# Attention and two feed-forward networks on one core: sums of weights one step ahead, g loads into x's buffers, conversions spread

## The chip, the core and the metric

One core of a Trainium2 chip runs the whole program once. The metric is the time of one execution on the device, in microseconds (us); lower is better. The engines of the core are TensorE (PE: matrix products, its loads of weights are shown as PEld), VectorE (DVE), ScalarE (ACT), GpSimd (POOL) and SyncE (SP), which issues nearly all DMAs of this kernel. Each engine takes its instructions in the order of the program.

## What is computed

```python
def reference(q, k, v, moe_w_in, moe_w_out, moe_alpha, moe2_w_in, moe2_w_out):
    # windowed attention: 4 batches, 8 heads, 576 positions, head size 64;
    # half of the heads see 32 keys, half see 32 keys at a dilation of 4
    attn = softmax(where(mask, q @ k.T / 8, -1e9)) @ v
    x = attn as (2304 tokens, 512)
    h = x @ moe_w_in                      # 512 x 2048
    x = (max(h, 0) + alpha * min(h, 0)) @ moe_w_out    # 2048 x 512
    h = x @ moe2_w_in
    g = where(h >= 1, h, where(h <= -1, 0, (h + 1) ** 2 / 4))
    return g @ moe2_w_out
```

## The kernel before

**Numbers.** Products keep nearly float32 precision: each operand is split into a high part (fp32r, a copy on ACT) and a low part (source minus high, on DVE or POOL), and each product is three matmuls, high x low, low x high, high x high. `two` (L328) does the split. The weights arrive in another format and are converted by three DVE operations on integers (`w_make`, L307) from a staging buffer `st` filled by `w_load`.

**Tiles.** Activations lie transposed in XA (512 features, 2304 tokens). Each network goes over the tokens in tiles (L45): the first in 512, 256, 512 (the plain tiles) and 1024 tokens, the second in 1024, 1024 and 256. A tile of 1024 is a pair: its first product is done by a scheme with seven products for a 2 x 2 block (`p_h`, L544), for which sums of the quarters of w_in are needed beside the weights themselves. A pair runs eight steps; step p makes h and g for f = 2p and 2p + 1 (f is one of 16 groups of 128 hidden features): 14 groups of three matmuls, then y of the two f of the step before, 12 matmuls each. g of the first 512 tokens of the pair stays on the chip (gh, gl); that of the second 512 goes to HBM (`g_keep`, gd). After the eight steps y of the second half runs over the 16 f, with gh and gl loaded back (`g_load`) and the next tile's operands (`x_seven`) made beside it. These passages from the steps to the second half of y are called boundary 1, 2 and 3 here, after the three pairs. The last tile of 256 tokens is done like a plain one.

**What runs beside what.** The attention of batch 0 is at the start; the other 18 groups of attention run between the slots of the plain tiles (`attention_point`, STARTS, STAGES). Conversions of weights are handed out a few operations at a time (`conv`, `ops` in `slot`). w_out of the second network is converted for the f in HELD within the plain tiles and stored in HBM, and for the others in the second half of the first pair, three operations per f (L1076); a load of the next st buffer is issued when a conversion ends (`more`). Each f needs woh and wol (high and low of w_out, `wo_split`), in two buffers each.

**Sums of weights.** `w_sums` (L376) makes them on POOL: four differences of quarters (ss), then two splits, and stores the split results in HBM (kept). Those of the first network are made during plain tile 2, those of the second during the first pair's steps; for that the whole w_in is fetched again (wf). `p_weights` fetches them for the next step (`w_fetch`) and splits the weights proper (`w_split`, low part on DVE in plain tile 2, on POOL later). `p_h` calls `after(0)` behind its first product and `after(1)` at its end.

**Order.** Nothing is reordered: each engine runs what the program emits for it, in that order. Waits come from buffers: a tile with a tag waits until the earlier tile of the same tag has been read for the last time. Buffers of 0.5 MB are handed round by lists of tags (x_free, st_free, r_free), first in, first out.

Of the kernel before, what the change touches and what calls it, by code (L numbers as in the profile page):

```python
# [22 lines left out]
P = 128  # L23
# [9 lines left out]
GS = 3  # L33
# [31 lines left out]
STARTS = (1, 6, 10, 14, 18, 22, 26, 30, 36, 42, 48, 54, 60, 65, 69, 73, 77, 81)  # L65
# [5 lines left out]
HELD = [f for f in range(NF) if f < 6 or f >= NF - 2]  # L71
# [15 lines left out]
def attention_then_two_ffns(ctx: ExitStack, tc: tile.TileContext, a0, aqk, av, w1i, w1o, w2i, w2o, alpha, masks, ident, out):  # L87
# [44 lines left out]
    def a_scores(i, pool, tag, add_on_pe):  # L132
# [15 lines left out]
        s = tmp(i).tile([P, 2 * GS, KEYS], F32, tag="s", name="s")  # L148
# [37 lines left out]
    def e_exp(i):  # L186
        ps = sc_t.pop(i)
        s = tmp(i).tile([P, 2 * GS, KEYS], F32, tag="s", name="s")
# [21 lines left out]
    def a_turn(i, pool, tag):  # L210
# [4 lines left out]
        pT = tmp(i).tile([P, GS, P], F32, tag="pT", name="pT")  # L215
# [138 lines left out]

    def w_split(n, f):
        t = r_slot((n, f))
        two(t[:, 0], t[:, 1], wi[n[0], f], nc.vector if n == PLAIN[2] or (n == PAIRS[0] and f < 2) else nc.gpsimd)
# [11 lines left out]

# [6 lines left out]
    def w_sums(ph, p):  # L376

        on = nc.gpsimd
        t, own = [], {}

        def fetch():
            own["tag"] = x_free.pop(0)
            own["w"] = pools[own["tag"]].tile([P, 2, DM], F32, tag=own["tag"], name="wf")
            nc.sync.dma_start(own["w"], whole[ph, 0, p])

        def quarter(i):
            w = (halves[p] if ph == 0 else own["w"])[:, i // 2]
            return w[:, (i % 2) * HW:(i % 2 + 1) * HW]

        def s12():  # L390
            t.append(ss_p.tile([P, 4, HW], F32, tag="ss", name="ss"))
            on.tensor_tensor(t[0][:, 0], quarter(3), quarter(2), ALU.add)
            on.tensor_tensor(t[0][:, 1], t[0][:, 0], quarter(0), ALU.subtract)

        def s34():
            on.tensor_tensor(t[0][:, 2], quarter(0), quarter(3), ALU.subtract)
            on.tensor_tensor(t[0][:, 3], quarter(1), t[0][:, 1], ALU.subtract)

        def keep(j):
            src = t[0][:, 2 * j - 2:2 * j].rearrange("p a b -> p (a b)")  # L400
            tag = x_free.pop(0)
            r = pools[tag].tile([P, 2, DM], F32R, tag=tag, name="wr")
            two(r[:, 0], r[:, 1], src, on)

            def store():
                kept[ph, p, j] = kept_p.tile([P, 2, DM], F32, tag=f"k{ph}_{p}_{j}", name="kept")
                nc.sync.dma_start(kept[ph, p, j], r.bitcast(F32))
                x_free.append(tag)

            later.append(store)  # L410

        def over():
            x_free.append(own["tag"])

        def save():
            d = kept_p.tile([P, 2, DM], F32, tag=f"fi_{p}", name="whole")
            nc.sync.dma_start(d, halves[p])
            whole[0, 0, p] = d

        if ph == 0:  # L420
            return [(s12, s34, save), (lambda: keep(1), lambda: keep(2), lambda: x_free.append(f"i{p}"))]
        return [(fetch,), (s12, s34, over), (lambda: keep(1), lambda: keep(2))]

    def w_fetch(key, n, p, j):
        t = r_slot(key)
        nc.sync.dma_start(t.bitcast(F32), kept[n[0], p, j])
        return t

    def p_weights(n, p, i):

        w_split(n, 2 * p + i)
        wt[n, p, 1 + i] = w_fetch((n, p, 1 + i), n, p, 1 + i)
# [70 lines left out]

    def wo_split(key, f):
# [39 lines left out]
    def p_h(q, p, after):  # L544
# [4 lines left out]
        r = [wt.pop(k) for k in ((n, 2 * p), (n, p, 1), (n, p, 2), (n, 2 * p + 1))]  # L549
# [59 lines left out]
        top(1, 1)  # L609
        product(d, 3, 0, 6, False)  # L610
# [8 lines left out]
        low(1, 1)  # L619
        top(0, 1)  # L620
        low(1, 0)
        low(0, 1)
        for k in ((n, 2 * p), (n, p, 1), (n, p, 2), (n, 2 * p + 1)):
            r_done(k)
        if p == NF // 2 - 1:
            x_free.extend(x_tags.pop(n))
        after(1)
# [7 lines left out]
    def g_load(n, f):  # L635
        hi = g_p.tile([P, TW], F32R, tag="gh", name="gh", bufs=4)
        lo = g_p.tile([P, TW], F32R, tag="gl", name="gl", bufs=4)
# [31 lines left out]
    def f_y(key, f):  # L669
# [13 lines left out]
        for c in range(NC):  # L683
# [4 lines left out]
            nc.tensor.matmul(o, wh[:, cs], gl[:, :w], start=False, stop=(f == NF - 1))  # L688
        if f == NF - 1:
# [18 lines left out]
    with tc.manual_schedule(), ExitStack() as late:  # L708
# [3 lines left out]
        e_in = [sp.tile([P, QK + GS * 4 * DS], F32, name=f"e_in{i}") for i in range(NGB)]  # L712

# [128 lines left out]
        def attention_point():  # L842
            nonlocal point, nxt
            for i in list(at):
                k = point - at[i]
                stages = STAGES[2 if 2 * NF <= at[i] < 4 * NF else i > NGB]
# [36 lines left out]
        sums = [w_sums(0, p) for p in range(NF // 2)]  # L883
        pend_2 = [(1, f, 0) for f in range(NF)] + [(1, f, 1) for f in HELD]
        after_n = dict(zip(order, order[1:] + [None]))

        def slot(n, f, k):
# [14 lines left out]
            if n in PLAIN[:2] and f == NF - 1:  # L902
                for c in range(NC):
                    x_split(nn, c)
            if k in (0, 1):
# [3 lines left out]
            elif n != LAST:  # L909
                ops = 3  # L910
# [12 lines left out]
            if n == PLAIN[2]:  # L923
                for x in sums[f // 2][f % 2]:
                    x()
                    if f < NF - 1:
                        flush()
# [6 lines left out]
            if n == PLAIN[2]:  # L934
                if f == NF // 2:
                    turn = iter(range(1 << 30))
                    x_work.extend(x_seven(nn, lambda: ps_a.tile([P, TW], F32, tag="w" if nxt < NG or at else "wa"[next(turn) % 2], name="room")))
                if f >= NF // 2:
                    more_x((2 if f < READY - 1 else 0) if f < READY else 5 if f < NF - 1 else len(x_work))
                if f == NF - 4:  # L940
                    w_base(0, 0)
                if f == NF - 3:
                    p_weights(nn, 0, 0)
                if f == NF - 1:
                    p_weights(nn, 0, 1)
                    w_base(0, 1)
                    flush()
# [12 lines left out]
        for n in PLAIN:  # L960
            for f in range(NF):
# [4 lines left out]
                if n == PLAIN[0] and f == NF - 1:  # L966
                    st_free.append(x_free.pop())
                    more()
                if n == PLAIN[1] and f == NF - 4:
                    spare += [0, 0]  # L970
                if n == PLAIN[2] and f == READY - 1:
                    assert nxt == NG and not at
                    x_free.extend(pools_q)
                if n == PLAIN[2] and f == NF // 2 - 1:
                    assert not pend_w and not todo and not cv, (pend_w, todo)
                    x_free.extend(st_free)
                    st_free.clear()

        second = [w_sums(1, p) for p in range(NF // 2)]

        def step(q, p):
            n = PAIRS[q]
            split_pending()

            def after(i):
                if p + 1 < NF // 2:
                    p_weights(n, p + 1, i)
                if i and p + 2 < NF // 2:
# [185 lines left out]
```

## Times and profile before

| | us |
|---|---|
| median of 3 runs | 914.38 |
| the 3 runs | 910.52, 914.38, 914.49 |
| profiled execution | 910.34 |
| its span | 908.5 |

| engine | busy us | share of the span |
|---|---|---|
| PE | 846.0 | 93% |
| PEld | 693.6 | 76% |
| DVE | 564.2 | 62% |
| POOL | 467.3 | 51% |
| ACT | 435.6 | 48% |

The span is what the profile covers, from the first instruction to the last. The mean granted clock of PE over it is 0.981 of full speed. Plain tile 1 runs from about 146 to 207 us of the span, plain tile 2 to about 318, the first pair's steps to 442, boundary 1 and the second half of y to 505; the second pair's boundary is at 625, the third's at 800.

### The profile page before, as it was taken

What the parts mean: (1) busy time and instruction counts of PE and PEld (TensorE: products, weight loads), DVE (VectorE), ACT (ScalarE), POOL (GpSimd) and SP (SyncE); (2) the same over time, 40 slices, a digit from 0 to 9 for tenths busy, and PEclk for the clock granted to TensorE, in tenths of its full rate; (3) what the DMA queues carried; (4) which work ended last, traced back from release to release, by engine and by line L of the source; (5) the groups of instructions that cost most, each with busy time, mean ns of one, the idle gap of its engine ahead of it and who ended that gap; (6) DMA issues with size and microseconds to landing.
All of it is one profiled execution on the core that took longest, in us unless ns stands there. A gap on an engine that the chain in (4) does not pass through costs nothing.

```text
span 908.5 us, 14621 instructions
## 1 busy us (share of the span) xinstructions
PE 846.0 (93%) x5328; PEld 693.6 (76%) x5330; DVE 564.2 (62%) x931; ACT 435.6 (48%) x809; POOL 467.3 (51%) x397
## 2 busy tenths in 40 slices
PE   6889998997999989999778999997999999969998
PEld 3667777886677868888566888886778888858898
DVE  4788886897776776565427777776317767630143
ACT  3545444554555564645424445453334545433365
POOL 3455554663657747676747233332473242327576
PEclk9999999999999999999979999999899999999999
DMA  7877736895773566775589654533674644256430
GB/s 283 251 228 227 216 104 216 253 273 149 254 246 147 183 250 248 269 299 219 188 298 318 252 186 170 184 127 106 223 255 146 226 172 175 94 191 238 161 106 24
DMA packets 73031, 185.23 MB, mean 204 GB/s; under 512 B 7552, under 2 KB 15360, under 8 KB 72960
## 3 DMA queue, kind: packets, MB, share of 16 engines
q1 hardware_dynamic: 72672, 184.14, 58.8%
q8 instruction: 42, 0.69, 0.3%
q14 instruction: 29, 0.24, 0.1%
q10 hardware_dynamic: 288, 0.16, 0.1%
HBM read 127.13 MB, written 57.15 MB: 203 GB/s over the span
## 4 chain that ended last, share of the span: by engine, by line
PE 65%; issue 9%; DVE 9%; POOL 7%; ACT 5%; DMA 4%; SPq 0%; ACTq 0%; POOLq 0%; DVEq 0%
PE y L686 11%; PE y L688 10%; PE y L687 10%; PE h_ps L559 6%; PE h_ps L561 6%; PE h_ps L560 6%; PE h_ps L529 4%; PE h_ps L531 4%; PE h_ps L530 4%; POOL wol L330 3%; POOL wr L330 2%; PE o_ps L225 2%; ACT wr L329 2%; DMA gh<-gd 1%; PE s_ps L147 1%
## 5 line engine op out<-in xcount | busy, mean ns | idle before, releaser
L330 POOL TENSOR_TENSOR wol<-wo,woh 128x512 fp32r<-128x512 f32 x159 | 205.9, 1303 | 145.3 <-ACT woh L329 144.6
L686 PE MATMUL y<-gh,wol 128*128 128x512 f32 (+1 forms) x636 | 242.8, 382 | 29.3 <-DMA gh<-gd 16.8
L687 PE MATMUL y<-gh,woh 128*128 128x512 f32 (+1 forms) x636 | 237.8, 374 | 0.0
L688 PE MATMUL y<-gl,woh 128*128 128x512 f32 (+1 forms) x636 | 237.5, 373 | 0.0
L330 POOL TENSOR_TENSOR wr<-wb,wr 128x512 fp32r<-128x512 f32 x62 | 80.2, 1294 | 183.2 <-ACT wr L329 183.2
L686 PEld LDWEIGHTS y<-gh,wol 128*128 128x128 f32 x636 | 121.8, 191 | 56.9 <-POOL wol L330 21.6
L329 ACT ACTIVATE woh<-wo 128x512 fp32r<-128x512 f32 x159 | 96.8, 626 | 112.6 <-PE y L688 97.4
L688 PEld LDWEIGHTS y<-gl,woh 128*128 128x128 f32 x636 | 121.7, 191 | 21.9 <-DMA gl<-gd 0.7
L687 PEld LDWEIGHTS y<-gh,woh 128*128 128x128 f32 x636 | 122.0, 192 | 19.6
L559 PE MATMUL h_ps<-xv,wr 128*128 128x512 f32 x336 | 131.3, 391 | 3.2 <-DVE gl L667 1.4
L561 PE MATMUL h_ps<-xv,wr 128*128 128x512 f32 x336 | 130.8, 389 | 0.0
L560 PE MATMUL h_ps<-xv,wr 128*128 128x512 f32 x336 | 130.8, 389 | 0.0
L529 PE MATMUL h_ps<-xv,wr 128*128 128x512 f32 (+1 forms) x256 | 91.6, 358 | 2.0 <-DVE g L654 1.8
L530 PE MATMUL h_ps<-xv,wr 128*128 128x512 f32 (+1 forms) x256 | 87.2, 341 | 0.2 <-DVE xv L330 0.2
L531 PE MATMUL h_ps<-xv,wr 128*128 128x512 f32 (+1 forms) x256 | 87.2, 341 | 0.0
L573 ACT ACTIVATE g<-g,half 128x512 f32<-128x512 f32 x64 | 44.9, 723 | 71.6 <-DVE g L572 69.6
L559 PEld LDWEIGHTS h_ps<-xv,wr 128*128 128x128 f32 x336 | 63.1, 188 | 18.3 <-DVE gl L667 2.3
L561 PEld LDWEIGHTS h_ps<-xv,wr 128*128 128x128 f32 x336 | 63.1, 188 | 13.1
L560 PEld LDWEIGHTS h_ps<-xv,wr 128*128 128x128 f32 x336 | 63.1, 188 | 12.9
L330 POOL TENSOR_TENSOR wr<-wi,wr 128x512 fp32r<-128x512 f32 x32 | 41.4, 1294 | 52.1 <-ACT wr L329 51.6
L529 PEld LDWEIGHTS h_ps<-xv,wr 128*128 128x128 f32 x256 | 49.3, 192 | 11.1 <-issue 4.6
L601 DVE TENSOR_TENSOR u<-h_ps,u 128x512 f32<-128x512 f32 x24 | 16.6, 691 | 66.0 <-PE h_ps L561 47.7
(118 smaller groups left out, 1283.8 us busy)
## 6 DMA issues: line engine op xcount, KB each, us to landing
wr<-kept SPq DMA_DIRECT2D x48, 512.0 KB, 4.1
gd<-XA SPq DMA_DIRECT2D x48, 512.0 KB, 3.0
kept<-wr SPq DMA_DIRECT2D x32, 512.0 KB, 2.6
wb<-whole SPq DMA_DIRECT2D x32, 512.0 KB, 4.8
gh<-gd SPq DMA_DIRECT2D x48, 256.0 KB, 3.5
gl<-gd SPq DMA_DIRECT2D x48, 256.0 KB, 3.9
st<-w1i SPq DMA_DIRECT2D x16, 512.0 KB, 4.6
st<-w1o SPq DMA_DIRECT2D x16, 512.0 KB, 5.0
```

The costliest lines, as they stand in the source:

```text
L329: nc.scalar.activation(hi, src, AF.Copy)
L330: low_on.tensor_tensor(lo, src, hi.bitcast(F32), ALU.subtract)
L529: nc.tensor.matmul(ps[:, :w], r[:, 1, cs], x[:, 0, xs], start=(c == 0), stop=False)
L530: nc.tensor.matmul(ps[:, :w], r[:, 0, cs], x[:, 1, xs], start=False, stop=False)
L531: nc.tensor.matmul(ps[:, :w], r[:, 0, cs], x[:, 0, xs], start=False, stop=(c == NC - 1))
L559: nc.tensor.matmul(o, w[:, 1, cs], x[:, 0], start=start and m == 0, stop=False, skip_group_check=not start)
L560: nc.tensor.matmul(o, w[:, 0, cs], x[:, 1], start=False, stop=False, skip_group_check=not start)
L561: nc.tensor.matmul(o, w[:, 0, cs], x[:, 0], start=False, stop=m == 1, skip_group_check=not start)
L573: nc.scalar.activation(t, t, AF.Square, bias=half, scale=0.5)
L686: nc.tensor.matmul(o, wl[:, cs], gh[:, :w], start=(f == 0), stop=False)
L687: nc.tensor.matmul(o, wh[:, cs], gh[:, :w], start=False, stop=False)
L688: nc.tensor.matmul(o, wh[:, cs], gl[:, :w], start=False, stop=(f == NF - 1))
```

## The change

1. Sums: `w_sums` and `w_fetch` are gone. `p_weights` is called in four parts per step for the next step's weights: split of the first weight and the four differences, the two splits of the sums, split of the second weight. In the first pair nothing of it is stored; in the second the results are stored (kept), and the third pair fetches them. r buffers are released as their last product has been issued, and `after` is called a third time inside `p_h`.
2. `g_load` takes one buffer of x for both parts and issues one DMA. In the last step of a pair the first three f are loaded, and y of one f is issued within that step.
3. woh and wol get a third buffer each outside the plain tiles (attention's s and pT), and `wo_split` runs two f ahead in the second half of y.
4. HELD has six f instead of eight. They are converted in the first pair's steps, three operations each step; plain tile 1 converts one operation per slot instead of three. The others (ten) are converted in the second half of y, one f earlier than before.
5. In the plain tiles: the whole w_in of the first network is stored for p = 2 to 7 in plain tile 1 (`w_save`); the low parts of plain tile 2's weights move from DVE to POOL; plain tile 2's x splits are one in each of the last four slots, on POOL; `x_seven` begins one slot later; the starts and stages of attention shift by a point.

```diff
-STARTS = (1, 6, 10, 14, 18, 22, 26, 30, 36, 42, 48, 54, 60, 65, 69, 73, 77, 81)
+STARTS = (1, 6, 10, 14, 18, 22, 26, 30, 37, 43, 49, 55, 61, 66, 70, 74, 78, 82)
-HELD = [f for f in range(NF) if f < 6 or f >= NF - 2]
+HELD = [f for f in range(NF) if f < 4 or f >= NF - 2]
...
-        two(t[:, 0], t[:, 1], wi[n[0], f], nc.vector if n == PLAIN[2] or (n == PAIRS[0] and f < 2) else nc.gpsimd)
+        two(t[:, 0], t[:, 1], wi[n[0], f], nc.vector if n == PAIRS[0] and f < 2 else nc.gpsimd)
...
-    def w_sums(ph, p):
+    sums = {}
+    def p_weights(n, p, i):
         on = nc.gpsimd
...
+        def other(j):
+            t = wt[n, p, j] = r_slot((n, p, j))
+            if n == PAIRS[2]:
+                nc.sync.dma_start(t.bitcast(F32), kept[p, j])
+                return
+            two(t[:, 0], t[:, 1], sums[n, p][:, 2 * j - 2:2 * j].rearrange("p a b -> p (a b)"), on)
+            if n == PAIRS[1]:
+                kept[p, j] = kept_p.tile([P, 2, DM], F32, tag=f"k{p}_{j}", name="kept")
+                nc.sync.dma_start(kept[p, j], t.bitcast(F32))
+        if i == 0:
+            w_split(n, 2 * p)
+            if n != PAIRS[2]:
+                t = sums[n, p] = ss_p.tile([P, 4, HW], F32, tag="ss", name="ss")
+                on.tensor_tensor(t[:, 0], quarter(3), quarter(2), ALU.add)
+                on.tensor_tensor(t[:, 1], t[:, 0], quarter(0), ALU.subtract)
+                on.tensor_tensor(t[:, 2], quarter(0), quarter(3), ALU.subtract)
+                on.tensor_tensor(t[:, 3], quarter(1), t[:, 1], ALU.subtract)
+        elif i < 3:
+            other(i)
+        else:
+            w_split(n, 2 * p + 1)
...
     def wo_split(key, f):
-            hi = ws_p.tile([P, DM], F32R, tag="oh", name="woh")
-            lo = ws_p.tile([P, DM], F32R, tag="ol", name="wol")
+            pool, tags = ws_p, ("oh", "ol")
+            if n not in PLAIN:
+                turns.append(f)
+                if len(turns) % 3 == 0:
+                    pool, tags = s_p, ("s", "pT")
...
     p_h, after the fifth of its seven products and at its end:
+        r_done(keys[1])
+        r_done(keys[0])
+        after(1)
         product(d, 3, 0, 6, False)
...
         low(1, 1)
+        between(2)
         top(0, 1)
+        between(1)
         low(1, 0)
         low(0, 1)
...
-        after(1)
+        after(2)
...
     def g_load(n, f):
-        nc.sync.dma_start(hi.bitcast(F32), gd[n, f][:, 0])
-        nc.sync.dma_start(lo.bitcast(F32), gd[n, f][:, 1])
-        gt[(n, 1), f] = (hi, lo)
+        tag = x_free.pop(0)
+        t = pools[tag].tile([P, 2, TW], F32R, tag=tag, name="gx")
+        nc.sync.dma_start(t.bitcast(F32), gd[n, f])
+        gt[(n, 1), f] = (t[:, 0], t[:, 1])
...
     slot:
-            if n in PLAIN[:2] and f == NF - 1:
+            if n == PLAIN[0] and f == NF - 1:
                 for c in range(NC):
                     x_split(nn, c)
+            if n == PLAIN[1] and f >= NF - NC:
+                x_split(nn, f - NF + NC, True)
-                ops = 3
+                ops = 1 if n == PLAIN[1] else 3
...
     step, after(i):
+                if not end:
+                    for k in ((0,), (1, 2), (3,))[i]:
+                        p_weights(n, p + 1, k)
                 if i == 0:
+                    if p + 2 < NF // 2:
+                        w_base(n[0], p + 2)
                     flush()
+                    if end:
+                        for f in range(3):
+                            g_load(n, f)
+                elif i == 1 and end:
+                    one_y()
+                    wo_split((n, 0), NF - 2)
...
     after the steps of a pair:
+            wo_split((n, 0), NF - 1)
+            one_y()
+            wo_split((n, 1), 0)
+            one_y()
+            wo_split((n, 1), 1)
...
     second half of y, at each f:
-                while loaded < min(f + 4, NF):
+                if loaded < NF:
                     g_load(n, loaded)
                     loaded += 1
-                if f + 1 < NF:
-                    wo_split((n, 1), f + 1)
+                if f + 2 < NF:
+                    wo_split((n, 1), f + 2)
...
-                    else:
+                    if f + 1 not in HELD:
                         conv(3)
```

## Rows read from the trace of the kernel before

**Rows 1.** The page's head: the span, and each engine's busy time.
```profile
span 908.5 us, 14621 instructions
PE 846.0 (93%) x5328; PEld 693.6 (76%) x5330; DVE 564.2 (62%) x931; ACT 435.6 (48%) x809; POOL 467.3 (51%) x397
```

**Rows 2.** Stretches within first and second pair's steps: from:to, length, engines, clock, DMA.
```profile
340.00:430.00 90.00, 90.00 (x398) 74.52 (x398) 53.04 (x78) 49.62 (x92) 60.68 (x59) 1.00 0.69 260
510.00:610.00 100.00, 100.00 (x443) 82.81 (x442) 75.38 (x119) 52.82 (x88) 31.22 (x25) 1.00 0.46 169
```

**Rows 3.** PE's timeline at boundary 1: start, length; [idle before, its releaser].
```profile
446.39 0.50 PE L686 MATMUL y<-gh,wol 128*128 128x512 f32 x1 [3.51 <-POOL wol L330]
459.40 0.77 PE L686 MATMUL y<-gh,wol 128*128 128x512 f32 x1 [7.24 <-DMA gh<-gd]
485.04 0.50 PE L686 MATMUL y<-gh,wol 128*128 128x512 f32 x1 [0.90 <-POOL wol L330]
498.35 0.50 PE L686 MATMUL y<-gh,wol 128*128 128x512 f32 x1 [1.96 <-POOL wol L330]
```

**Rows 4.** Stretches behind gaps; the last three columns: PE clock, DMA share, GB/s.
```profile
459.40:465.40 6.00, 6.00 (x15) 4.51 (x16) 0.00 (x0) 0.33 (x1) 0.00 (x0) 0.53 0.83 290
498.35:503.35 5.00, 5.00 (x15) 3.95 (x16) 2.48 (x4) 0.29 (x1) 1.20 (x1) 0.66 1.01 397
637.30:643.30 6.00, 5.98 (x16) 4.62 (x17) 0.00 (x0) 0.48 (x1) 0.30 (x1) 0.57 0.75 259
218.70:223.70 5.00, 5.00 (x36) 3.85 (x37) 2.27 (x4) 1.04 (x2) 1.05 (x1) 0.66 1.00 290
```

**Rows 5.** PE's timeline at boundaries 2 and 3.
```profile
627.15 0.50 PE L686 MATMUL y<-gh,wol 128*128 128x512 f32 x1 [1.76 <-POOL wol L330]
637.32 0.77 PE L686 MATMUL y<-gh,wol 128*128 128x512 f32 x1 [4.42 <-DMA gh<-gd]
675.12 0.50 PE L686 MATMUL y<-gh,wol 128*128 128x512 f32 x1 [1.68 <-POOL wol L330]
813.14 0.73 PE L686 MATMUL y<-gh,wol 128*128 128x512 f32 x1 [5.10 <-DMA gh<-gd]
```

**Rows 6.** SP's timeline of DMA issues at boundary 1: start, issue time.
```profile
453.40 1.28 SPq L638 DMA_DIRECT2D gh<-gd  x1
...
480.07 0.33 SPq L274 DMA_DIRECT2D st<-w2o  x1
...
499.76 0.33 SPq L274 DMA_DIRECT2D st<-w2o  x1
```

**Rows 7.** Timeline of the second pair's last step: its tail and wol.
```profile
620.47 0.39 PE L686 MATMUL y<-gh,wol 128*128 128x512 f32 x1
624.64 0.60 ACT L588 ACTIVATE XA<-h_ps 128x512 fp32r<-128x512 f32 x1 [0.77 <-DVE h_ps L581]
625.27 0.69 DVE L593 TENSOR_TENSOR XA<-h_ps,XA 128x512 fp32r<-128x512 f32 x1
625.83 2.51 POOL L330 TENSOR_TENSOR wol<-wo,woh 128x512 fp32r<-128x512 f32 x2 [11.15 <-ACT woh L329]
```

**Rows 8.** POOL's timeline in a step of the first pair.
```profile
431.43 2.53 POOL L330 TENSOR_TENSOR wol<-wo,woh 128x512 fp32r<-128x512 f32 x2
...
436.13 0.73 POOL L397 TENSOR_TENSOR ss<-wf,ss 128x256 f32<-128x256 f32 x1
```

**Rows 9.** PE's and DVE's timeline from plain tile 1 to plain tile 2.
```profile
209.52 0.55 PE L214 MATMUL t_ps<-idt,s 128*128 128x128 f32 x3 [2.29 <-ACT XA L258]
218.04 0.56 DVE L233 TENSOR_TENSOR o<-o_ps,rs 128x384 f32<-128x384 f32 x1
218.70 1.02 PE L147 MATMUL s_ps<-qk 128*32 128x128 f32 x24 [3.65 <-issue]
```

**Rows 10.** Groups by line: low parts of weights; count, busy, mean ns, idle before.
```profile
L330 POOL TENSOR_TENSOR wr<-wi,wr 128x512 fp32r<-128x512 f32 x32 | 41.4, 1294 | 52.1 <-ACT wr L329 51.6
L330 DVE TENSOR_TENSOR wr<-wi,wr 128x512 fp32r<-128x512 f32 x16 | 13.3, 828 | 5.5 <-ACT wr L329 5.2
```

More of the change, by code (lines that the diff above doesn't have):

```diff
@@ L374, in flush @@
             later.pop(0)()
-    def w_sums(ph, p):
+    sums = {}
+    def p_weights(n, p, i):
         on = nc.gpsimd
[L379 to L422, printed above, removed]
@@ L510, in wo_split @@
         else:
-            hi = ws_p.tile([P, DM], F32R, tag="oh", name="woh")
-            lo = ws_p.tile([P, DM], F32R, tag="ol", name="wol")
+            pool, tags = ws_p, ("oh", "ol")
[3 more added lines that the diff above has]
+                    pool, tags = s_p, ("s", "pT")
+            hi, lo = (pool.tile([P, DM], F32R, tag=t, name=m) for t, m in zip(tags, ("woh", "wol")))
         two(hi, lo, wo[n[0], f], nc.gpsimd)
@@ L542, in banks, with p_h @@
         return [(ps_h, "h"), (ps_h, "h"), (ps_a, "w"), (ps_a, "a")]
-    def p_h(q, p, after):
+    def p_h(q, p, after, between):
         n = PAIRS[q]
@@ L712, in attention_then_two_ffns, with buf @@
         e_in = [sp.tile([P, QK + GS * 4 * DS], F32, name=f"e_in{i}") for i in range(NGB)]
+        def buf(i, tag):
+            n = GS * P
+            if i < NGB and i % 2:
+                return sp.tile([P, n], F32, tag=tag, name=tag)
+            return s_p.tile([P, TW], F32, tag=tag, name=tag)[:, :n]
         def tmp(i):
@@ L881, in one_y @@
             f_y(*pend_y.pop(0))
-        sums = [w_sums(0, p) for p in range(NF // 2)]
-        pend_2 = [(1, f, 0) for f in range(NF)] + [(1, f, 1) for f in HELD]
+        pend_2 = [(1, f, 0) for f in range(NF)]
         after_n = dict(zip(order, order[1:] + [None]))
@@ L965, in attention_then_two_ffns @@
                     spare += [0, 0]
[L966 to L970, printed above, removed]
+                if n == PLAIN[1]:
+                    if 2 <= f < NF // 2:
+                        w_save(f)
+                    if f == NF - 4:
+                        base.update({(0, p): [f"i{p}", 4 if p < 2 else 2] for p in range(NF // 2)})
                 if n == PLAIN[2] and f == READY - 1:
                     assert nxt == NG and not at
-                    x_free.extend(pools_q)
-                if n == PLAIN[2] and f == NF // 2 - 1:
                     assert not pend_w and not todo and not cv, (pend_w, todo)
-                    x_free.extend(st_free)
+                    x_free.extend(st_free + pools_q)
                     st_free.clear()
-        second = [w_sums(1, p) for p in range(NF // 2)]
         def step(q, p):
@@ L1011, in attention_then_two_ffns @@
                 pend_y += [((n, 0), 2 * p), ((n, 0), 2 * p + 1)]
-            split_pending()
+            assert not pend_w and not todo and not cv
             flush()
-            if q == 0:
-                for x in second[-1][1] + second[-1][2]:
-                    x()
+            wo_split((n, 0), NF - 1)
[3 more added lines that the diff above has]
+            wo_split((n, 1), 1)
             turn = iter(range(1 << 30))
@@ L1024, in attention_then_two_ffns @@
                 w0_tile[0] = room
-                for _ in range(2):
-                    st_free.append(x_free.pop())
                 rest = [(1, f, 1) for f in range(NF) if f not in HELD]
@@ L1074, in attention_then_two_ffns @@
                         nc.sync.dma_start(wo[1, f], whole[1, 1, f // 2][:, f % 2])
[L1075 removed]
+                    if f + 1 not in HELD:
                         conv(3)
[L1077 to L1082 removed]
+                    if f == NF - 4:
+                        assert not pend_w and not todo and not cv
+                        x_free.extend(st_free)
+                        st_free.clear()
         for f in range(NF):
```

112 lines of the change are left out of this document (51 added, 61 removed).

## The prediction

> **What bounds the kernel now.** I read the head of the page first: TensorE (PE) is busy 93% of a 908.5 us span [rows 1]. So no other engine's total can be the bound, and the question is only where PE stands still or runs at the lower of its two clocks (1.2 instead of 2.4 GHz, granted 0.5). The second view is the table of stretches over the steps of the three paired tiles: PE is busy for every microsecond at full clock, a 512-column matmul starts every 0.226 us (90 us / 398), and POOL is used 67% in the first pair and 31% in the second [rows 2]. A step has 66 matmuls, so 15.0 us; nothing is to be won inside the steps, only to be lost. The third view is the timeline of PE, of which I kept the gaps over 0.6 us, and the stretches behind them. The time lies at four places.
>
> - Boundary 1, from the first pair's steps to its second half of y: gaps of 3.51, 7.24, 0.90 and 1.96 us [rows 3], sum 13.6. Behind the second the clock is 0.53 for 6.0 us and behind the last 0.66 for 5.0 us [rows 4]: 6.0 x 0.47 + 5.0 x 0.34 = 4.5 lost. In all 18.1 us.
> - Boundary 2 (second pair): 1.76 + 4.42 + 1.68 [rows 5], and 6.0 x 0.43 = 2.6 of clock [rows 4]: 10.4 us.
> - Boundary 3 (third pair): 5.10 [rows 5], a gap like boundary 2's first (two such stand in the trace, 1.76 and 1.77), and about 1.7 of clock (I take the 5 us at 0.66 [rows 4]): 8.6 us.
> - From plain tile 1 to plain tile 2: 2.29 + 3.65 [rows 9] and 5.0 x 0.34 = 1.7 of clock [rows 4]: 7.6 us.
>
> Sum 44.7 us of the span. The long gap of each boundary ends with the landing of gh from gd; SP issued that load only at 453.40, in the middle of the gap [rows 6], since gh and gl have four buffers that the steps themselves use until their last y.
>
> **Boundaries, loads of g.** The change issues the first three g loads, one DMA each instead of two, in the last step, into buffers of x, some 19 us ahead of their use (84 matmuls by 0.226); gd of these f was stored six steps earlier. The waits of 7.24, 4.42 and 5.10 us go, and the half clock behind them. What is late next is wol of f = 15: its hi copy stands on ACT behind the step's last top copy, which ends 4.77 us after the first y matmul of the tail (620.47 to 625.24), and wol then ends near 627.1, 6.7 us after it [rows 7]. In the new order y of f = 12 runs inside the last step and y of 13 and 14 fill 24 x 0.226 = 5.4 us of these. So 1.2 us stay at each boundary, where 1.8 to 3.5 stood. The second kind of wait, wol in the second half of y (0.90, 1.96, 1.68 us), comes from woh having two buffers and being made one f ahead; with three buffers and two ahead it has 5.4 us of cover instead of 2.7. At boundaries 2 and 3 I cost it at nothing; without that cover the old 1.7 us come back.
> Gain of boundary 2: 10.4 - 1.2 = 9.2. Of boundary 3: 8.6 - 1.2 = 7.4.
>
> **Boundary 1, second half of y.** Here the conversions of w_out run: ten weights now (f = 4 to 13) instead of eight, one per f from f = 3, three DVE operations each, fed from two staging buffers. In the trace the six loads of st after the first two are issued from 480.07 to 499.76, one every 3.94 us [rows 6], while an f takes 12 x 0.226 = 2.7 us. So the conversions fall behind, DVE stalls in order, then the x products behind it, then ACT's woh, then POOL's wol; and SP's next w_load waits for DVE with the next g_load queued behind it. DMA asks for ten gd, eight st, one base and two stored sums of 0.524 MB over ten f: 11.0 MB in 27 us, 405 GB/s, where the rows give 290 GB/s at share 0.83 and 397 at 1.01 [rows 4], that is 350 to 393 at most. POOL has a burst too: sums (four of 0.73, [rows 8]) and lo copies (1.29, [rows 10]) of the next tile at f = 8 to 11, some 1.8 us more than its cover. Against this stand three g in advance and two wol in advance. Bounds for what stays: nothing, if the cover holds, and 8 x (3.94 - 2.7) = 9.9 plus 1.7 of clock, if PE is paced by the conversions. The trace of before is nearest to the low end (2.9 us of gaps with one f of cover and the same kind of queue), so I take 4.0. Boundary 1 keeps 1.2 + 4.0, gain 18.1 - 5.2 = 12.9.
> The Trainium skill ("DMA: Bandwidth & Descriptors", Specifications) puts the limit of HBM for one core at about 358 GB/s; by it, as an estimate, the 11.0 MB take 30.7 us, 3.4 more than ten f. The trace does not agree: it has 5 us at 397 GB/s [rows 4].
>
> **Plain tiles.** Plain tile 1 gets one conversion operation per slot instead of three (16 instead of 48, 0.69 us each on DVE, 22 us), since only w_in and no w_out of the second network is converted there; the held w_out go to the first six steps of the first pair. The four x splits at the tile's end go to POOL, one in each of the last four slots, and the lo parts of plain tile 2's weights go from DVE to POOL: 16 x 0.83 = 13 us off DVE, 16 x 1.29 = 21 us onto POOL [rows 10]. From POOL go the network-1 sums and their lo parts in this tile, 8 x (4 x 0.73 + 2 x 1.29) = 44 us, so POOL gets lighter. The gap of 2.29 us is ACT's four xv copies ahead of a_out: it goes. The gap of 3.65 is labelled issue, but s_ps takes the PSUM bank that the last DVE operation of a_norm reads at 218.04 for 0.56 us, and PE starts at 218.70 [rows 9]: it is DVE's backlog. With that backlog gone I leave 1.0 of the 7.6 us: gain 6.6 (bounds 2.3, the ACT gap alone, and 9, with small waits inside tile 1 as well). Six 0.5 MB stores of w_in move to plain tile 1; some ten fewer st loads make room on SP's queue.
> The Trainium skill ("GPSIMD Engine Reference", Engine selection) puts elementwise two-input work on VectorE. By it this move is a loss: 0.46 us an operation, 7.4 us in all [rows 10]; it costs that only where POOL ends last, and here PE waits for DVE [rows 9].
>
> **Steps.** In the first pair the sums are made for the next step from the weights at hand, the same POOL work as before (67% [rows 2]), without the stored and fetched copies. In the second pair POOL gets four sums and two lo parts more, 5.5 us a step, 4.7 + 5.5 = 10.2 of 15.0. New order on POOL from the tail on: lo 1.29, two wol 2.53 [rows 8], lo 1.29, four sums 2.94, so the sums end 8.0 us after the tail's copies plus one hi copy of 0.6, about 8.6 us into the next step. ACT reaches the hi copies of the sums after four products (5.4) and five operations of 0.6 to 0.73 us, at 8.9. So ACT hardly waits, and the two copies delay the tail by 0.6 to 1.2 us. Its last DVE operation ends at 625.96 [rows 7], 0.1 us after the next step's start at T + 5.4, and its bank is wanted 4.1 us into it: over 2.8 us of cover. Three conversion operations per step (2.1 us) in the first pair lie before the tail's last three DVE operations and take most of that cover. I cost the steps at nothing; upper bound 0.5 us x 15 = 7. Below nothing is excluded, as PE has no idle time there [rows 2]. The rotation of r buffers releases each before its next writer, by one product or more.
>
> **Sum.** 12.9 + 9.2 + 7.4 + 6.6 = 36.1 us. The profiled execution took 910.34 us (span 908.5 and 1.8 around it): 874.2. The three runs shown lie from 910.52 to 914.49 with a median of 914.38, so I apply the share, 36.1 / 910.34 = 4.0%, to the median: 878.
>
> **Rivals.**
> - Boundary 1 is paced by the conversions: 11.6 stay instead of 4.0, 7.6 us less gained, 885. For it: the 3.94 us of an st load, and 405 GB/s asked. Against it: the deeper cover. By the limit in the Trainium skill ("DMA: Bandwidth & Descriptors", Specifications) it would be the likelier one; the row with 397 GB/s [rows 4] speaks against that.
> - The gap of 3.65 us is not DVE's backlog: of 7.6 only 2.3 go, 882.
> - The prefetch does not come early: SP takes DMAs in order, and a g load queued behind a wait for a free x buffer, a kept store or an st load lands as late as now. Then 7.24 + 4.42 + 5.10 and the clock behind them (7.1) stay: 24 us, 902. Against it: in the last step SP has little else to do, and x buffers are freed by then.
> - Slower: the sums hold ACT up in each of the 15 steps. ACT is in order, and act, top and low of a step stand behind the hi copies of the sums. The tail's cover of 2.8 us is used when the sums end 3.1 us later than I worked out, 11.7 us into the step. From 2.4 us beyond that (15 x 2.4 = 36) the whole gain is given back; with twice that, 4.8 us a step, it is 36 slower than before, 950. For it: POOL's share in the second pair doubles and its place in the chain moves to the middle of the step. Against it: the first pair has 67% of POOL today and loses nothing.
>
> **How the numbers follow.** My forecast 0.53, the paced boundary 0.19, the issue gap 0.10, the late prefetch 0.07, the sums in ACT's way 0.11 (0.04 near no change, 0.07 slower). Measurements of this kernel tell 0.5% from no change, so faster is under 909.8: 0.89; same 0.04; slower 0.07. The range goes from all covers holding (boundary 1 keeps 1.2, plain tiles gain 9: 43 us, 871, and the lowest run of before lies 4 lower: 867) to the paced boundary with 7 us of steps and the plain tiles' low bound (7.6 + 7 + 4.3 more: 897): 866 to 896.
>
> **What would show it.** Right: no PE gap over 2 us at the three boundaries, the first g loads issued by SP within the last step, steps still 15.0 us with PE busy throughout, no half clock between plain tiles 1 and 2, and in boundary 1's second half gaps of 3 to 6 us that end on wol or g. Wrong: DVE waiting for st of w2o with PE gaps every f; ACT waiting for ss in the steps and steps of over 15.5 us; g loads issued behind a wait on SP.

## The result, and the profile after

| | us |
|---|---|
| before, median of 4 runs | 913.85 (910.52 to 914.49) |
| after, median of 4 runs | 883.17 (881.87 to 885.16) |
| ratio, 95% interval | 0.967 (0.964 to 0.970) |
| forecast | 878 (866 to 896) |

The change is faster by 3.3%, 30.7 us. The profiled execution of the changed kernel took 881.87 us, its span is 880.1, so 28.4 us of span against the 36.1 of the sum. The head of the page after, and its row of clocks by slices, answer to [rows 1]:

```profile
span 880.1 us, 14306 instructions
PE 839.0 (95%) x5328; PEld 688.4 (78%) x5330; DVE 552.8 (63%) x911; ACT 433.6 (49%) x809; POOL 487.8 (55%) x417
PEclk9999999999999999999999999999999999999999
```

PE does the same 5328 matmuls, and no slice's clock falls below 0.9 any more, though one shorter stretch does (below). PE's timeline of the changed kernel, the gaps that answer to [rows 3, 5, 9] (start, length, [idle before, releaser]; L679 is the old L686):

```profile
138.97 0.86 PE L147 MATMUL s_ps<-qk 128*32 128x128 f32 x24 [3.28 <-issue]
214.56 0.55 PE L214 MATMUL t_ps<-idt,s 128*128 128x128 f32 x3 [2.73 <-ACT XA L258]
445.66 0.50 PE L679 MATMUL y<-gh,wol 128*128 128x512 f32 x1 [0.99 <-POOL wol L330]
475.05 0.47 PE L679 MATMUL y<-gx,wol 128*128 128x512 f32 x1 [1.52 <-DMA gx<-gd]
482.50 0.47 PE L679 MATMUL y<-gx,wol 128*128 128x512 f32 x1 [1.69 <-DMA gx<-gd]
616.79 0.50 PE L679 MATMUL y<-gh,wol 128*128 128x512 f32 x1 [1.61 <-POOL wol L330]
782.92 0.50 PE L679 MATMUL y<-gh,wol 128*128 128x512 f32 x1 [1.50 <-POOL wol L330]
```

The gaps of 7.24, 4.42 and 5.10 us on gh are gone; wol of the last f stays, and in the first pair's second half two gaps on gx. The first two lines are in the plain tiles, and the first of them is new. The second stands at the place of the 2.29 us of [rows 9], and behind it the clock falls, with 0.66 granted over 5 us:

```profile
214.56:219.56 5.00, 5.00 (x18) 4.06 (x19) 0.00 (x0) 1.02 (x3) 2.41 (x2) 0.66 0.02 3
```

SP's timeline after, against [rows 6]: the first g loads are issued in the last step, and in the second half a g load stands behind an st load:

```profile
426.71 0.51 SPq L624 DMA_DIRECT2D gd<-XA  x1
427.32 2.66 SPq L629 DMA_DIRECT2D gx<-gd  x3
...
470.62 0.33 SPq L274 DMA_DIRECT2D st<-w2o  x1
471.00 0.43 SPq L629 DMA_DIRECT2D gx<-gd  x1
```

The stretches that answer to [rows 2], in the first and the second pair's steps, and most of the first pair's second half (busy times of PE, PEld, DVE, ACT and POOL; the last three columns are clock, DMA share, GB/s):

```profile
340.00:430.00 90.00, 90.00 (x397) 74.20 (x396) 62.48 (x94) 49.12 (x91) 64.21 (x62) 1.00 0.44 148
510.00:600.00 90.00, 90.00 (x397) 74.20 (x396) 65.14 (x102) 52.38 (x91) 62.84 (x61) 1.00 0.49 178
448.50:492.00 43.50, 39.52 (x169) 31.15 (x168) 30.70 (x45) 18.88 (x35) 35.52 (x29) 1.00 0.86 312
```

Where the time went is read from the first copy of a tile's y to XA, one mark per tile. The plain tiles' marks before and after:

```profile
148.66 0.60 ACT L695 ACTIVATE XA<-y 128x512 f32<-128x512 f32 x1 [0.50 <-PE y L688]
224.46 0.39 ACT L695 ACTIVATE XA<-y 128x256 f32<-128x256 f32 x1 [1.89 <-PE y L688]
338.16 1.08 ACT L695 ACTIVATE XA<-y 128x512 f32<-128x512 f32 x2
```
```profile
152.63 0.60 ACT L690 ACTIVATE XA<-y 128x512 f32<-128x512 f32 x1 [0.52 <-PE y L681]
225.56 0.65 ACT L690 ACTIVATE XA<-y 128x256 f32<-128x256 f32 x2
337.82 1.08 ACT L690 ACTIVATE XA<-y 128x512 f32<-128x512 f32 x2
```

| stretch, mark to mark | before | after | difference | forecast |
|---|---|---|---|---|
| start and plain tile 0 | 148.66 | 152.63 | +4.0 | 0 |
| plain tile 1 | 75.80 | 72.93 | -2.9 | |
| plain tile 2 | 113.70 | 112.26 | -1.4 | -6.6 for tiles 1 and 2 |
| first pair | 182.72 | 169.89 | -12.8 | -12.9 |
| second pair | 175.14 | 165.84 | -9.3 | -9.2 |
| third pair | 163.43 | 157.37 | -6.1 | -7.4 |
| last tile | 44.66 | 44.59 | -0.1 | 0 |

The pairs came out within 1.4 us each. The plain tiles won next to nothing: 0.3 us in place of 6.6, as what tiles 1 and 2 won (4.3) was lost in tile 0.

### The profile page after: what moved, and what is told of

It is laid out like the page before. It is cut to its first block, busy times and chain, and to the rows that moved or that the text cites. A ratio compares the mean times of both kernels' runs of the same rounds, so it can differ in the third digit from the quotient of the medians.

```text
span 880.1 us, 14306 instructions
## 1 busy us (share of the span) xinstructions
PE 839.0 (95%) x5328; PEld 688.4 (78%) x5330; DVE 552.8 (63%) x911; ACT 433.6 (49%) x809; POOL 487.8 (55%) x417
## 4 chain that ended last, share of the span: by engine, by line
PE 83%; DVE 7%; ACT 4%; issue 2%; POOL 1%; DMA 1%; ACTq 0%; DVEq 0%
PE y L679 13%; PE y L681 13%; PE y L680 13%; PE h_ps L545 8%; PE h_ps L547 8%; PE h_ps L546 8%; PE h_ps L514 5%; PE h_ps L516 4%; PE h_ps L515 4%; PE o_ps L225 2%; PE s_ps L147 1%; PE t_ps L214 1%; POOL wol L330 1%; ACT woh L329 1%; DMA st<-w2o 1%
## 5 line engine op out<-in xcount | busy, mean ns | idle before, releaser
L679 PE MATMUL y<-gh,wol 128*128 128x512 f32 (+1 forms) x444 | 163.7, 369 | 4.8 <-POOL wol L330 4.8
L681 PE MATMUL y<-gl,woh 128*128 128x512 f32 (+1 forms) x444 | 160.3, 361 | 0.0
L680 PE MATMUL y<-gh,woh 128*128 128x512 f32 (+1 forms) x444 | 160.1, 361 | 0.0
L330 POOL TENSOR_TENSOR wr<-wi,wr 128x512 fp32r<-128x512 f32 x50 | 64.7, 1295 | 101.4 <-ACT wr L329 101.3
L679 PEld LDWEIGHTS y<-gh,wol 128*128 128x128 f32 x444 | 83.8, 189 | 21.8 <-POOL wol L330 7.4
L681 PEld LDWEIGHTS y<-gl,woh 128*128 128x128 f32 x444 | 83.7, 188 | 13.3
L680 PEld LDWEIGHTS y<-gh,woh 128*128 128x128 f32 x444 | 83.8, 189 | 12.2
L679 PE MATMUL y<-gx,wol 128*128 128x512 f32 x192 | 75.6, 394 | 4.0 <-DMA gx<-gd 3.2
L680 PE MATMUL y<-gx,woh 128*128 128x512 f32 x192 | 75.3, 392 | 0.0
L545 PEld LDWEIGHTS h_ps<-xv,wr 128*128 128x128 f32 x336 | 63.1, 188 | 15.6 <-POOL wr L330 1.3
L681 PE MATMUL y<-gx,woh 128*128 128x512 f32 x192 | 75.3, 392 | 0.0
L547 PEld LDWEIGHTS h_ps<-xv,wr 128*128 128x128 f32 x336 | 63.1, 188 | 13.2
```

What stands on the lines that cost most here:

```text
L330: low_on.tensor_tensor(lo, src, hi.bitcast(F32), ALU.subtract)
L545: nc.tensor.matmul(o, w[:, 1, cs], x[:, 0], start=start and m == 0, stop=False, skip_group_check=not start)
L547: nc.tensor.matmul(o, w[:, 0, cs], x[:, 0], start=False, stop=m == 1, skip_group_check=not start)
L679: nc.tensor.matmul(o, wl[:, cs], gh[:, :w], start=(f == 0), stop=False)
L680: nc.tensor.matmul(o, wh[:, cs], gh[:, :w], start=False, stop=False)
```

## Experiments

The kernel before ran beside each group; ratios are to it. The changed kernel itself had 0.967 in the result and, run once more beside others, 0.971 (0.968 to 0.973):

> The changed kernel as it is, so that the others of this group stand beside it on one chip: 0.967 of the kernel before, about 881 where the kernel before takes 910.6.

It took 884.87 us. The others are held against 0.967 to 0.971.

**The points of attention.** The question was why plain tile 0 lost 4 us although none of its own work had changed. Four versions change only where groups of attention start and how their stages lie.

```diff
-stages = STAGES[2 if 2 * NF <= at[i] < 4 * NF - 4 else 0 if i in (NGB, 2 * NGB) else 1]
+stages = STAGES[2 if 2 * NF <= at[i] < 4 * NF - 4 else i > NGB]
```

> The changed kernel (883.17 us) with one thing back: attention group 12 uses the stages of the groups behind it (values two points before the next group's scores) as in the kernel before, so its values no longer fall on the point at which group 13's scores start. Theory S (the gap labelled issue is the shared PSUM bank: scores of the next group are emitted right behind the values of the last and wait for DVE to read them): the gap of 3.28 us at 139 goes, plain tile 0 ends 4 us earlier, 879. Theory D (it is DVE's backlog at the end of a plain tile, whatever the points): the gap stays, 883.

878.01 us, 0.964 (0.962 to 0.967). The gap at 139 is gone and plain tile 0's mark is at 147.66 instead of 152.63. Theory S holds for this gap. DVE's timeline of the changed kernel shows what the label issue hides: the four low parts of the next tile's x, and only then a_norm's reads of the PSUM bank for which s_ps at 138.97 waits.

```profile
134.75 3.22 DVE L330 TENSOR_TENSOR xv<-XA,xv 128x256 fp32r<-128x256 f32 x4 [1.10 <-ACT xv L329]
137.90 0.15 DVE L231 TENSOR_SCALAR rs<-o_ps 128x6 f32<-128x6 f32 x1
138.09 0.19 DVE L232 RECIPROCAL rs<-rs 128x6 f32<-128x6 f32 x1
138.31 0.56 DVE L233 TENSOR_TENSOR o<-o_ps,rs 128x384 f32<-128x384 f32 x1
```

Two things come together here: values and next scores on one point, and work queued on DVE ahead of the read. The next version takes the old points and stages:

```diff
-STARTS = (1, 6, 10, 14, 18, 22, 26, 30, 37, 43, 49, 55, 61, 66, 70, 74, 78, 82)
+STARTS = (1, 6, 10, 14, 18, 22, 26, 30, 36, 42, 48, 54, 60, 65, 69, 73, 77, 81)
-stages = STAGES[2 if 2 * NF <= at[i] < 4 * NF - 4 else 0 if i in (NGB, 2 * NGB) else 1]
+stages = STAGES[2 if 2 * NF <= at[i] < 4 * NF else i > NGB]
```

> The changed kernel with the start points and stages of attention of the kernel before. Theory S: the gap at 139 goes (4 us), and a gap comes back between plain tile 1 and plain tile 2, where values and scores fall on one point again; as DVE is lighter there than before, it is about 1 to 2 us instead of 3.65 and the clock stays up: 879 to 881. Theory D: no gap between plain tiles 1 and 2 (DVE has no backlog there now), the gap at 139 stays: 883.

875.13 us, 0.961 (0.959 to 0.963), better than expected. PE's gap at the place of [rows 9]:

```profile
214.85 0.42 PE L147 MATMUL s_ps<-qk 128*32 128x128 f32 x7 [1.59 <-issue]
```

1.59 us where the same points gave 3.65 with the old load on DVE, and no lower clock. The marks of plain tiles 1 and 2 are at 219.04 and 329.47: with the old points the rest of the change wins 8.7 us in the plain tiles, 7.7 of them in tiles 1 and 2 (tile 0's mark is at 147.68). The smaller waits of t_ps for XA count too: PE's gaps over 0.6 us from 130 to 332 us sum to 15.1 in the changed kernel and to 7.8 here.

```diff
-STARTS = (1, 6, 10, 14, 18, 22, 26, 30, 37, 43, 49, 55, 61, 66, 70, 74, 78, 82)
+STARTS = (1, 6, 10, 14, 18, 22, 26, 30, 36, 42, 48, 54, 60, 65, 69, 73, 77, 81)
-stages = STAGES[2 if 2 * NF <= at[i] < 4 * NF - 4 else 0 if i in (NGB, 2 * NGB) else 1]
+stages = STAGES[2 if 2 * NF <= at[i] < 4 * NF - 4 else i > NGB]
```

> The changed kernel with the start points of the kernel before, group 12 in the later stages, and the earlier switch of stages (groups that start from point 60 on are short) kept, so that nowhere do values and scores fall on one point. Theory S: neither gap, 877 to 879. Theory D: as the changed kernel, 883, and the gap at 139 stays.

878.2 us, 0.964 (0.962 to 0.966): inside theory S's numbers, but worse than the version before it, so my list of collisions was too short. Group 17's output and group 18's transposes now share a point, as they do in the changed kernel (2.73 at 214.56):

```profile
207.47 0.75 PE L214 MATMUL t_ps<-idt,s 128*128 128x128 f32 x3 [2.72 <-ACT XA L258]
```

The last of this row keeps these apart too:

```diff
+stages = STAGES[0 if i == 3 * NGB else 2 if 2 * NF <= at[i] < 4 * NF else i > NGB]
```

> The changed kernel with the start points of attention of the kernel before, its stages, and one group (18) on the short stages, so that neither values and next scores nor output and next transposes fall on the same point of the program. Theory S2 (any two uses of the one PSUM bank at the same point cost PE the read between them): the gap of 1.6 us labelled issue and that of 1.3 us on XA between plain tiles 1 and 2, which the version with the old points had, go too: 2 to 3 us less than that version (0.961 of the kernel before), 0.958. Rival (those gaps are DVE's and ACT's load): as that version, 0.961.

874.92 us, 0.959 (0.954 to 0.964). The interval holds both numbers; whether it beats the old points isn't told. Of the gaps named, 1.29 and 1.15 us stay, so they are not removed by points alone:

```profile
208.21 0.44 PE L214 MATMUL t_ps<-idt,s 128*128 128x128 f32 x2 [1.29 <-ACT XA L258]
214.89 0.86 PE L147 MATMUL s_ps<-qk 128*32 128x128 f32 x24 [1.15 <-issue]
```

This version differs from the one before it in the stages of group 18 alone. So of the 2.72 us there, 1.4 come from the shared point; what the other 1.3 wait for was not tested.

**The early load of g.**

```diff
-                    if end:
-                        for f in range(3):
-                            g_load(n, f)
...
-            loaded = 3
+            loaded = 0
...
-                if loaded < NF:
+                while loaded < min(f + 4, NF):
```

> The changed kernel with one part undone: the first g loads are issued at the start of the second half of y (four ahead from there on) and not in the last step; they still go into buffers of x in one DMA each. Theory A (the early load is what took the boundaries' long gaps away): PE waits for gx at each of the three boundaries for 4 to 7 us and runs at the lower clock behind it, 24 us in all as worked out for the kernel before, 905 to 909. Rival (y within the last step and wol two ahead would have covered most of it): 12 us or less, 895 or less.

909.86 us, 0.999 (0.997 to 1.001): nothing is left of the gain. PE's timeline, and the stretches behind the three gaps:

```profile
453.05 0.77 PE L679 MATMUL y<-gx,wol 128*128 128x512 f32 x1 [4.33 <-DMA gx<-gd]
636.42 0.77 PE L679 MATMUL y<-gx,wol 128*128 128x512 f32 x1 [6.39 <-DMA gx<-gd]
812.16 0.76 PE L679 MATMUL y<-gx,wol 128*128 128x512 f32 x1 [6.53 <-DMA gx<-gd]
```
```profile
453.05:458.05 5.00, 5.00 (x12) 3.95 (x13) 0.00 (x0) 0.00 (x0) 0.57 (x1) 0.50 1.03 411
636.40:642.40 6.00, 5.97 (x14) 4.74 (x15) 0.00 (x0) 0.42 (x1) 0.00 (x0) 0.50 1.03 419
812.10:817.10 5.00, 4.94 (x13) 3.92 (x14) 0.00 (x0) 0.00 (x0) 0.00 (x0) 0.55 1.02 412
```

The three gaps sum to 17.3 us, and after each PE runs for 5 to 6 us at or near 1.2 GHz (granted 0.50 to 0.55), which loses 7.8 more: 25 of the 28 us by which this profile's span is longer than the changed kernel's. Theory A holds. The converse, the kernel before with this part alone:

```diff
     def g_load(n, f):
-        hi = g_p.tile([P, TW], F32R, tag="gh", name="gh", bufs=4)
-        lo = g_p.tile([P, TW], F32R, tag="gl", name="gl", bufs=4)
-        nc.sync.dma_start(hi.bitcast(F32), gd[n, f][:, 0])
-        nc.sync.dma_start(lo.bitcast(F32), gd[n, f][:, 1])
+        tag = x_free.pop(0)
+        t = pools[tag].tile([P, 2, TW], F32R, tag=tag, name="gx")
+        nc.sync.dma_start(t.bitcast(F32), gd[n, f])
...
+                    if p == NF // 2 - 1:
+                        for f in range(3):
+                            g_load(n, f)
```

> The kernel before with one part alone: g is loaded into one buffer of x by one DMA, the first three in the last step of the pair, one per f behind that; two r buffers are lent to x for the second half of y. Theory A (this part is most of the gain): the gaps on gh of 7.24, 4.42 and 5.10 us and most of the lower clock behind them (7.1) go, wol's gaps stay: 17 to 24 us less than the kernel before, 887 to 894. Rival (without the third woh buffer and two ahead PE waits for wol at the same place, so the time comes back): 8 us less at most, 903 or more.

897.02 us, 0.984 (0.982 to 0.986): 14.6 us, between both theories. At each boundary PE's timeline has the next wait in the place of the old one:

```profile
455.12 0.50 PE L689 MATMUL y<-gx,wol 128*128 128x512 f32 x1 [1.86 <-POOL wol L331]
629.28 0.50 PE L689 MATMUL y<-gx,wol 128*128 128x512 f32 x1 [1.87 <-POOL wol L331]
799.49 0.50 PE L689 MATMUL y<-gx,wol 128*128 128x512 f32 x1 [1.87 <-POOL wol L331]
```

So without the early load nothing of the gain is left, and alone (with one DMA in place of two and the two lent buffers) it brings about half of it. The other half needs the rest of the change too; this version shows waits on wol, 5.6 us in these three lines, that the changed kernel does not have there.

**woh, wol and the second half of y.**

```diff
-                turns.append(f)
-                if len(turns) % 3 == 0:
-                    pool, tags = s_p, ("s", "pT")
```

> The changed kernel with two buffers of woh and wol everywhere instead of three. Theory W (the third buffer is the cover in the second half of y): ACT waits for y of f before it may copy woh of f + 2, PE waits for wol at the boundaries for 2 to 4 us each and up to 1 us at many f: 8 to 25 us more than the changed kernel, 889 to 906. Rival (with g early, two buffers suffice): within 2 us of the changed kernel.

888.4 us, 0.975 (0.970 to 0.979), its runs 884.1 to 891.27. Theory W's 8 to 25 us are wrong: against 884.87 on the same chip it is 3.5 us, and the intervals overlap. Its profile has two gaps on wol of 0.46 us in the second pair's second half, where W wanted up to 1 at many f, and 1.07, 1.61 and 1.61 at the boundaries, where W wanted 2 to 4; the changed kernel has 0.99, 1.61 and 1.50.

```profile
620.46 0.50 PE L677 MATMUL y<-gh,wol 128*128 128x512 f32 x1 [1.61 <-POOL wol L330]
648.54 0.50 PE L677 MATMUL y<-gx,wol 128*128 128x512 f32 x1 [0.46 <-POOL wol L330]
```

```diff
                 if loaded < NF:
                     g_load(n, loaded)
                     loaded += 1
+                hold = False
+                more()
+                hold = True
```

> The changed kernel; in the second half of y of the first pair each load of st is issued behind the next g load instead of ahead of it. Theory Q (the two gaps on gx, 1.52 and 1.69 us, come because SP holds the g load behind an st load that waits for DVE): both go, 3 us less than the changed kernel, 878. Rival R (the DMA engines are full there, whatever the order): the gaps stay or move, within 1 us of the changed kernel.

884.03 us, 0.970 (0.967 to 0.973), 0.8 us from the changed kernel on the same chip. Theory Q falls as to time: no gap on gx is left, but gaps on wol stand at the same place.

```profile
484.01 0.50 PE L679 MATMUL y<-gx,wol 128*128 128x512 f32 x1 [0.75 <-POOL wol L330]
488.04 0.50 PE L679 MATMUL y<-gx,wol 128*128 128x512 f32 x1 [0.98 <-POOL wol L330]
493.00 0.62 PE L679 MATMUL y<-gx,wol 128*128 128x512 f32 x1 [1.93 <-POOL wol L330]
```

On the version with the points apart, the last woh copy was then emitted ahead of the step's last top copy:

```diff
+            def between(k):
+                if end and k == 2:
+                    wo_split((n, 0), NF - 1)
+                if q == 0:
+                    conv(k)
...
-            wo_split((n, 0), NF - 1)
             one_y()
```

> As the version with the points kept apart, and the woh copy of the last f of a pair's first half is emitted ahead of the step's last top copy on ACT instead of behind it. Theory T (the 1.0 to 1.6 us that stay at each boundary are wol behind that copy): the gaps at the three boundaries shrink below 0.5 us, 3 to 4 us less than the version without it, 0.954 to 0.955 of the kernel before. Rival (y of this f then waits for its g, which is made last as well): within 1 us of it.

873.65 us, 0.958 (0.954 to 0.962), the lowest median here, 38 us under the kernel before on the same chip; against 874.92 it is 1.3 us, which the intervals don't tell apart. In its profile the gaps of 1.61 and 1.50 us at boundaries 2 and 3 are 0.28 and 0.17, followed by 0.58 and 0.51 at the next f: some 40% of what goes comes back one f later. At boundary 1 nothing is won, as the 0.99 us goes and 1.02 us stands at the next f.

```profile
441.77 0.50 PE L679 MATMUL y<-gx,wol 128*128 128x512 f32 x1 [1.02 <-POOL wol L330]
608.09 0.50 PE L679 MATMUL y<-gh,wol 128*128 128x512 f32 x1 [0.28 <-POOL wol L330]
614.48 0.50 PE L679 MATMUL y<-gx,wol 128*128 128x512 f32 x1 [0.58 <-POOL wol L330]
```

So the place of the wait is as theory T had it, at boundaries 2 and 3. Last, on top of this, the number of conversions in the second half:

```diff
-HELD = [f for f in range(NF) if f < 4 or f >= NF - 2]
+HELD = [f for f in range(NF) if f < 6 or f >= NF - 2]
...
-                        for f in range(3):
+                        for f in range(2 if q == 0 else 3):
```

> As the version before this one, and eight weights are converted in the first pair's steps instead of six, so eight and not ten in the second half of y (as many as in the kernel before); for the buffers this takes, only two g are loaded early in the first pair. Theory C (the 6 to 8 us that stay in the first pair's second half are the chain of conversions, since issuing the g loads first only moved the gaps from gx to wol): that stretch loses 3 to 4 us less, 0.950 to 0.951 of the kernel before. Rival (DMA engines full with the loads of g): no gain, 0.954.

877.48 us, 0.962 (0.957 to 0.966): no gain. The last two steps now convert as well, and wol pays at the boundary, while the second half has the same DMA rate with two conversions fewer:

```profile
446.52 0.50 PE L679 MATMUL y<-gx,wol 128*128 128x512 f32 x1 [3.19 <-POOL wol L330]
```
```profile
446.50:490.00 43.50, 40.16 (x160) 32.15 (x161) 28.08 (x39) 16.14 (x30) 33.95 (x28) 0.92 0.85 317
```

From mark to mark that second half takes 61.1 us, and 61.4 in the version it builds on. Theory C is not confirmed; it isn't refuted either, as one g load less is made early here.

**The low parts in plain tile 2.**

```diff
-nc.vector if n == PAIRS[0] and f < 2 else nc.gpsimd
+nc.vector if n == PLAIN[2] or (n == PAIRS[0] and f < 2) else nc.gpsimd
```

> The changed kernel (0.969 of the kernel before) with one part undone: in plain tile 2 the low parts of the weights go back from POOL (1.29 us each) to DVE (0.83 us). Theory D (DVE ends last in the plain tiles, so taking 13 us from it was worth something): 1 to 4 us more than the changed kernel, 0.970 to 0.974 of before, PE waiting for DVE in plain tile 2. By the rule on engine selection POOL is the wrong place, and it would be up to 7 us faster: 0.962. Third: PE has its cover in plain tile 2 either way, within 1 us of the changed kernel.

887.66 us, 0.973 (0.969 to 0.977); the interval overlaps those of the changed kernel, so by time alone it isn't settled. The marks of plain tiles 0 and 2 in its profile:

```profile
154.34 0.60 ACT L690 ACTIVATE XA<-y 128x512 f32<-128x512 f32 x1 [0.52 <-PE y L681]
340.97 1.08 ACT L690 ACTIVATE XA<-y 128x512 f32<-128x512 f32 x2
```

Plain tiles 1 and 2 together take 186.6 us between these marks and 185.2 in the changed kernel (185.0 in its second run), so 1.4 to 1.7 us more, and the gap of 2.73 us is one of 3.36. It is not faster, as it would be by the rule on engine selection in the Trainium skill ("GPSIMD Engine Reference", Engine selection), which puts this work on VectorE.

## Why the prediction was right, and where it was not

**Boundaries 2 and 3.** The mechanism, its place and its size held: forecast -9.2 and -7.4, measured -9.3 and -6.1. The gap left on wol was put at 1.2 us from [rows 7]; it is 0.99, 1.61 and 1.50. The third pair's term was 1.3 too large, of which 0.3 is this gap; for the rest I have no gap over 0.6 us, so it stays open.

**Boundary 1.** -12.8 against -12.9. The stay was put at 1.2 + 4.0; the gaps over 0.6 us are 0.99, and in the second half 1.52, 1.69 and one of 0.77, 4.0 in sum. That this size fits so well is partly luck: the 4.0 were a choice between bounds of 0 and 11.6, taken from 2.9 us of gaps in a kernel with other buffers. The cause as I gave it is only half shown: a g load does stand behind an st load, but with the order turned round the time stayed, and with two conversions (and one early g load) fewer it stayed too. What remains is DMA at 309 to 317 GB/s over the second halves of these three versions and the chain from DVE by ACT and POOL to wol; which of them ends last was not separated. The Trainium skill's limit for one core ("DMA: Bandwidth & Descriptors", Specifications, about 358 GB/s) does not decide it: behind the late g loads the same DMA engines moved 419 GB/s for 6 us.

**Plain tiles.** Here the prediction failed, by 6.3 us of the 7.7 by which its sum was too high. What it left out is a part of the change it didn't cost at all, the starts and stages of attention. They put group 12's values and group 13's scores on one point (3.28 us) and group 17's output and group 18's transposes on another (1.4 of 2.73). It also said of the gap of 2.29 us in [rows 9] that it goes: 2.73 stands in its place, and the sign "no half clock between plain tiles 1 and 2" did not come true (0.66 over 5 us). With the old points 1.28 us of it stays. Its reading of the gap of 3.65 us in [rows 9] is borne out: DVE's backlog, down to 1.59 with the same points once the work was gone, with no lower clock.

With the old points plain tiles 1 and 2 win 7.7 us, more than the forecast 6.6, and the kernel stands at 0.961; the sum had 36.1 / 910.34, that is 0.960. That this fits is partly luck. At the place of [rows 9] 1.28 + 1.59 us stay where 1.0 was left, so 4.7 us come from there; the others come from smaller waits in plain tile 2 that the sum did not hold (gaps over 0.6 us: 6.0 before, 1.8 with the old points). The time alone, 883.17 us, would also have fitted the rival at 882, that the gap of 3.65 us is not DVE's; it is the rows that speak against it.

**Steps.** Costed at nothing, and nothing it was: a matmul every 0.227 us in both pairs' steps, PE busy throughout, POOL in the second pair at 70% (62.84 of 90; forecast 10.2 of 15.0). The rival of the sums in ACT's way is out. No version undid the sums alone, so what they are worth by themselves, with the DMA of the first pair's steps down from 260 to 148 GB/s, is not shown. The rival of the late prefetch is out by SP's rows; its price of 24 us was a little low: that version stands at 0.999 against 0.967 to 0.971, 25 to 29 us.

**The low parts on POOL.** The sign is as forecast in the profiles, 1.4 to 1.7 us over plain tiles 1 and 2; the times alone don't prove it.

**The third woh buffer.** Costed as 0.90 and 1.96 us at boundary 1 and 1.68 at boundary 2. With two buffers the profile of the changed kernel has gaps on wol of 0.46 us twice in the second pair. It hides less than I gave it; the time differs by 3.5 us with overlapping intervals.

## What to carry to other kernels

Cost every edit of the change, the constants too: starts and stages shifted by a point, two of them so that a PSUM bank's reader and next writer met, ate some 7 us (0.969 to 0.961), and a wait labelled issue was such a bank. A wait that is taken away shows the next one in line; in the kernel before with the early load alone, 16.8 us of waits on DMA became 5.6 us of waits on wol. When a version moves a gap but not the time, look for what bounds the whole stretch, and say so if it isn't found.

## What the runs showed of the hardware

With the loads late, PE ran at the lower level (1.2 GHz, granted 0.50 in the stretch shown) for some 6 us behind a gap of 6.39 us, so this gap cost about 9. Behind the gaps of 0.99 to 1.69 us of the changed kernel's boundaries the matmuls kept the full clock. In between, the length of the gap did not decide it. The clock fell behind 1.96 us in the kernel before [rows 3, 4] and behind 2.73 us in the changed kernel, but not behind 3.51 us in the kernel before [rows 3]:

```profile
446.40:449.90 3.50, 3.50 (x15) 2.88 (x16) 0.00 (x0) 0.63 (x1) 3.42 (x5) 1.00 0.45 178
```

One gap of the changed kernel even did both. Behind the 3.28 us at 138.97 the clock stayed up in the result's profile, and behind the same gap (3.29 us at 140.23) it fell in the second run of this kernel:

```profile
139.00:145.00 6.00, 6.00 (x53) 5.13 (x54) 2.42 (x4) 2.46 (x5) 0.74 (x1) 1.00 0.61 171
140.23:146.23 6.00, 6.00 (x43) 4.84 (x44) 2.42 (x4) 2.44 (x5) 0.72 (x1) 0.72 0.56 158
```

Plain tile 0's mark is at 152.63 in the first and at 155.46 in the second; of these 2.8 us, 1.3 lie ahead of the gap, and the lower clock accounts for the rest (6 x 0.28 = 1.7 us). So two runs of one kernel can differ by that much.

And DMA reached 419 GB/s over 6 us when nearly all that was in flight were g loads of 0.5 MB (one load of weights was issued in that time), where the second half with its mixed loads and stores ran at 312.
